# Softcap attention and a gated convolution block on one core: the first six pairs' steps and the weights' fetches placed anew

## The chip, the cores and the metric

The kernel runs on one core of one Trainium2 chip. The core's engines work side by side, each on its own list of instructions in order: TensorE (PE, the matmuls), ScalarE (ACT), VectorE (DVE), GpSimd (POOL) and SyncE (SP), which here issues all the transfers between the chip's memory and the core's own memory (SBUF). Matmuls write into PSUM, eight banks of it. The metric is the device time of one execution in microseconds (us); less is better.

## The reference: what is computed

For 8 batches, 12 heads, a sequence of 448 and a head size of 64:

```
scores = cap * tanh(q @ k^T / 8 / cap)          # 448 x 448 for each head
attn   = exp(scores - max) ; attn /= sum(attn) + 1e-9
x      = attn @ v                               # heads side by side: 448 x 768 for each batch
gate   = sigmoid(sum over i < 5 of conv_w[i] * x shifted by i - 4 rows)
out    = (gate * (x @ w_val)) @ w_out
```

q, k, v and cap are 32-bit floats; w_val, w_out (768 x 768 each) and conv_w (5 x 768) come as 64-bit floats, 8 bytes an element.

## The kernel before

Work goes by pairs of heads: 48 pairs, six to a batch. q and k come in blocks of 32 x 32 and are turned on DVE (`turn`, L296). `scores` (L317) gives four tiles a pair, each 112 keys by 448 queries for both heads; `tanh` (L325) and `exp` (L329) are ACT's. `attnv` (L354) multiplies exp'd tiles with v, and `sums` (L366) multiplies them with ones, which gives the denominators. DVE then turns the sums (L374), takes the reciprocal (L380, L381), spreads it (L387) and multiplies (L395): the result u is x for this pair, channels on partitions. `x_hi` (L400, ACT) and `x_lo` (L236, DVE) cut x into a leading and a remaining part. `conv` forms the gate's sum: its first product is ACT's (L412) for the first eleven pairs, the four others are DVE's (L416). For each batch there follow the value projection `val` (L437 to L439, three matmuls for each part of a product), the sigmoids (L422), the gate product (L443), and the output projection `out_part` (L466 to L468).

[...] Twelve steps of 256 rows by 384 columns (six for w_val, six for w_out) convert them during the first eleven pairs. A step fetches the same numbers twice (`weight_load`): as pairs of 32-bit words (`w_raw`, L270) and shifted by 16 bits (`w_late`, L271), in two pieces of 384 KB each. Then `float64_split` works in three parts: `first` is ACT's L136 and L137 on the raw copy, and DVE's L138 on the late copy; `second` is DVE's L141 and L142, which reads the raw copy for the last time; `third` is L145 and L146, which reads the late copy for the last time. There is one buffer for each copy and one for the work tile `w_t`, so a fetch for the next step must wait for L142 (raw) or L146 (late).

The order of the instructions on every engine is written out by hand. A table gives each step of a pair a time in units of a pair (`"tanh": (0.0, 0.01, 0.51, 0.52)` for the four tiles of pair p means p + 0.0 and so on); all steps of all pairs, with the weights' steps (`W_AT`), projections (`VAL_FIRST`, `OUT_EVEN` and so on) and sigmoids, are sorted by these times, and the engines' lists are made in that order. An engine takes its instructions in this order and waits at each until its inputs are there. There is no other planner: the times set the order alone.

Table `EARLY` serves pairs 0 to 4 and `HANDED` pair 5; pairs 6 to 10 have `PAIRED`, then `STEADY`, then `SPLIT`. In `EARLY`, pair p's ACT order is tanh 0, 1, exp 0, 1, tanh 2, 3, exp 2, 3, and then x_hi and the first convolution product of pair p-1. PE's is scores 2 and 3 of p, products and sums of tiles 2 and 3 of p-1, scores 0 and 1 of p+1, products and sums of tiles 0 and 1 of p. From pair 6 on, DVE first adds tiles two by two (L339), so that two sums a pair are left.

PSUM has two buffers for scores, each of two banks, two banks for products and sums of even pairs and, in the first six pairs, two (shared with the projections) for those of odd pairs (`bank`).

Of the kernel before, what the change touches and what calls it, by code (L numbers as in the profile page):

```python
# [10 lines left out]
U16 = mybir.dt.uint16  # L11

AF = mybir.ActivationFunctionType
ALU = mybir.AluOpType
# [7 lines left out]
P = 128  # L22
# [11 lines left out]
WC = 2  # L34
# [6 lines left out]
STEADY = {  # L41
    "load_q": -1.9,
    "load_k": -1.85,
    "load_v": -0.6,
    "tq": -0.90,
    "tk": -0.85,
    "scores": (0.0, 0.05, 0.62, 0.67),
    "tanh": (0.06, 0.13, 0.68, 0.75),
    "exp": (0.22, 0.29, 0.82, 0.89),
# [12 lines left out]
SPLIT = STEADY | {"q_hi": -0.69, "k_hi": -0.68, "q_lo": -0.475, "k_lo": -0.47}  # L62
PAIRED = STEADY | {"add": (0.52, 1.03), "sums": (1.28, 1.29)}
EARLY = {
    "load_q": -1.9,
    "load_k": -1.85,
    "load_v": -0.6,
    "tq": -0.78,
    "tk": -0.72,
    "scores": (-0.31, -0.30, 0.19, 0.20),  # L70
    "tanh": (0.0, 0.01, 0.51, 0.52),
    "exp": (0.17, 0.18, 0.68, 0.69),
    "av": (0.84, 0.95, 1.33, 1.46),
    "sums": (0.85, 0.96, 1.34, 1.47),
    "turn_sums": 1.60,
    "recip": 1.62,
    "spread": 1.65,
    "mul": 1.72,
    "x_hi": 1.87,
    "x_lo": 1.90,  # L80
    "conv": (1.88, 1.99, 2.06, 2.12, 2.18),
}

HANDED = EARLY | {
    "av": (0.84, 0.95, 1.06, 1.08),
    "sums": (0.85, 0.96, 1.07, 1.09),
    "turn_sums": 1.30,
    "recip": 1.32,
    "spread": 1.34,
    "mul": 1.40,  # L90
    "x_hi": 1.42,
    "x_lo": 1.46,
    "conv": (1.44, 1.54, 1.58, 1.70, 1.74),
}

LATE_X = {"x_lo": 1.76, "conv": (1.78, 1.80, 1.83, 1.86, 1.89)}
NEARLY, NPAIRED, NPLAIN = 6, 11, 13

VAL_FIRST = (6.50, 6.85, 7.36, 7.74, 8.36, 8.74)
VAL = (6.85, 7.36, 7.74, 8.36, 8.74, 9.36)  # L100
SIG_FIRST, SIG_AT = 7.15, 7.44
OUT_EVEN = (9.80, 10.36, 10.74, 11.36, 11.74, 12.36)
OUT_ODD = (9.80, 10.36, 10.74, 10.80, 11.36, 11.74, 11.80, 12.36)
OUT_LATE = (9.80, 10.36, 10.74, 11.74, 12.36, 12.60)
PART = 0.13
KEEP_AT = 10.2
W_AT = (0.93, 1.95, 2.9, 3.7, 4.5, 5.35, 7.1, 8.1, 9.1, 9.9, 10.6, 11.15)
W_LOAD = -0.5
W_SECOND, W_THIRD = 0.02, 0.05
W_FREE = 11.3  # L110
CW_LOAD, CW_AT = -0.55, 0.7
EPS = 1e-9


def words(ap):

    return ap.bitcast(I32).rearrange("p (n two) -> p n two", two=2)


def shifted(t, n):  # L120


    return t.bitcast(I32)[..., 1:2 * n:2]


def float64_split(nc, raw, mid, hi, lo, t):

    tf = t.bitcast(F32)
    top = raw[..., 1].bitcast(F32)

    def first():
        nc.scalar.activation(tf, top, AF.Copy, scale=2.0 ** -112)  # L136
        nc.scalar.sign(top, top)  # L137
        nc.vector.tensor_scalar(mid, mid, 0x01FFFFFF, None, ALU.bitwise_and)  # L138

    def second():  # L140
        nc.vector.tensor_scalar(t, t, 0x0FFFFE00, 3, ALU.bitwise_and, ALU.logical_shift_left)  # L141
        nc.vector.tensor_tensor(hi, tf, top, op=ALU.mult)  # L142

    def third():
        nc.vector.tensor_scalar(t, hi.bitcast(I32), -0x00800000, None, ALU.bitwise_and)  # L145
        nc.vector.scalar_tensor_tensor(lo, mid, 2.0 ** -36, tf, ALU.mult, ALU.mult)  # L146

    return first, second, third
# [39 lines left out]
def load_v(nc, pool, v, p):  # L188

    _, H, S, D = v.shape  # L190
    b, hp = divmod(p, H // 2)
    vn = pool.tile([CH, 2, S // CH, D], F32, name="vn")
    for j in range(2):
        nc.sync.dma_start(vn[:, j], v[b, 2 * hp + j].rearrange("(t r) d -> r t d", r=CH))
    return vn


def fast_path(tc, io, u2, q, k, v, w_val, conv_w, w_out, out, capt):
# [5 lines left out]
    nc = tc.nc  # L204
# [3 lines left out]
    NP = B * NPAIR  # L208
# [5 lines left out]
    NH = DM // 2  # L214
# [6 lines left out]
    with ExitStack() as ctx:  # L221
# [28 lines left out]
        for t in u2:  # L250
# [5 lines left out]
        wsteps = [  # L256
            (w, slice(c, c + WC), nh, t) for w, t in ((w_val, wv), (w_out, wo)) for nh in range(2) for c in range(0, NCC, WC)
        ]
        wstate = {}
# [3 lines left out]
        def weight_load(n):  # L263
            w, c, nh, _ = wsteps[n]
            raw = wsc.tile([P, WC, NH, 2], I32, name="w_raw", bufs=RB)
            late = wsc.tile([P, WC, 4 * NH + 2], U16, name="w_late", bufs=RB)
            for i in range(WC):
                r = (c.start + i) * P
                src = w[r:r + P, nh * NH:(nh + 1) * NH]
                nc.sync.dma_start(raw[:, i], words(src))  # L270
                nc.sync.dma_start(late[:, i, 1:1 + 4 * NH], src.bitcast(U16))  # L271
            wstate[n] = raw, shifted(late, NH)

        def weight_first(n):
            _, c, nh, w = wsteps[n]
# [18 lines left out]
        def turn(name, p):  # L294
            t = wk.tile([P, S], F32, name=name + "t")
            nc.vector.transpose(t, loads.pop((name, p)))  # L296
            state.setdefault(p, {})[name] = t
# [182 lines left out]
        stored = {}  # L480
        cw_steps = []
        events = []
        tables = [EARLY if p < NEARLY - 1 else HANDED if p < NEARLY else PAIRED if p < NPAIRED else STEADY if p < NPLAIN else SPLIT for p in range(NP)]
        for p in range(NPLAIN, NP):
            if p % NPAIR == 0:
                tables[p] = tables[p] | LATE_X
# [1 line left out]
        def at(when, f, *a):  # L488
            events.append((when, len(events), f, a))
# [4 lines left out]
            load_v=lambda p: vloads.update({p: load_v(nc, io, v, p)}),  # L494
            tq=lambda p: turn("q", p), tk=lambda p: turn("k", p),
            q_hi=lambda p: half_hi("q", p), k_hi=lambda p: half_hi("k", p),
            q_lo=lambda p: half_lo("q", p), k_lo=lambda p: half_lo("k", p),
            scores=scores, tanh=tanh, exp=exp, add=add, av=attnv, sums=sums, turn_sums=turn_sums, recip=norm_recip,
            spread=spread, mul=norm_mul, x_hi=x_hi, x_lo=x_lo, conv=conv,
        )  # L500
        for p, table in enumerate(tables):
            for name, f in steps.items():
                x = table.get(name, ())
# [5 lines left out]
        for b in range(B):  # L509
            t0 = NPAIR * b  # L510
# [14 lines left out]
            for m, y in enumerate(OUT_ODD if b % 2 else OUT_LATE if b == B - 2 else OUT_EVEN):  # L525
# [2 lines left out]
                at(t0 + y + 0.20, store, b, m)  # L528
                at(t0 + y + 0.40, store_out, b, m)
        for n, t0 in enumerate(W_AT):  # L530
            at(W_AT[n - 1] + W_THIRD if n else W_LOAD, weight_load, n)
            at(t0, weight_first, n)
            at(t0 + W_SECOND, weight_second, n)
            at(t0 + W_THIRD, weight_third, n)
        at(W_FREE, free_scratch)
        at(CW_LOAD, lambda: cw_steps.append(load_conv_w(nc, wsc, conv_w, cw)))
        at(CW_AT, lambda: cw_steps[0]())
# [129 lines left out]
def kernel(tc, q, k, v, cap, w_val, conv_w, w_out, out):  # L667
    nc = tc.nc
    with tc.tile_pool(name="cap_pool", bufs=1) as pool, tc.tile_pool(name="io", bufs=2) as io:
        capt = pool.tile([P, 1], F32, name="capt")  # L670
        nc.sync.dma_start(capt, cap.rearrange("(o c) -> o c", o=1).partition_broadcast(P))

        pad = conv_w.shape[0] - 1
        u2 = [pool.tile([P, pad + q.shape[2]], F32, name=f"u{i}") for i in range(2)]
        for t, src in zip(u2, (q, k)):
            load_blocks(nc, t[:, pad:], src, 0)
        mag = pool.tile([1, 1], F32, name="mag")
        nc.vector.scalar_tensor_tensor(mag, capt[0:1], -1.0, capt[0:1], ALU.mult, ALU.max)
        small = pool.tile([1, 1], I32, name="small")
        nc.vector.tensor_scalar(small, mag, CAP_FAST, None, ALU.is_le)  # L680
        flag = nc.values_load(small, min_val=0, max_val=1)
        with tc.If(flag != 0) as cmp:
            fast_path(tc, io, u2, q, k, v, w_val, conv_w, w_out, out, capt)
        with cmp.Else():
            general_path(tc, q, k, v, w_val, conv_w, w_out, out, capt)
# [30 lines left out]
```

## Time and profile before

| what | value |
|---|---|
| median of 3 runs | 774.95 us (773.33 to 777.27) |
| the profiled execution | 775.05 us, its span 773.3 us |
| mean granted clock of PE | 0.988 |
| busy share of the span | PE 95%, DVE 77%, ACT 70%, POOL 1% |
| HBM read, written | 51.94 MB, 11.01 MB |

A row of a timeline has the start from the span's beginning and the duration, both in us, then engine, line, operation, output and inputs, the shape and the count of instructions merged into the row; in brackets stands the engine's idle time just before it and who ended it. A row of waits has the waiting engine and line, what it waited for, and total us, count, and longest. A row of windows has for each engine the busy us and the instructions that began in the window; its last three columns are PE's granted clock, the share of the DMA engines' time, and GB/s. A row of DMA issues ends with KB each and median us from issue to landing. PE and PEld are the matmul and the weight-loading side of TensorE; a 32-bit matmul shows as two records, so one tile of scores for two heads is x4. PE's ends are modelled, so a busy PE need not be at its peak.

### The profile page before, as it was taken

The page shows a single profiled execution, that of the slowest core. Times are in us where ns is not written, and L with a number is a line of the kernel's source. Part 1 is how long each engine was busy: PE and PEld are TensorE (multiplying, and loading weights), DVE is VectorE, ACT ScalarE, POOL GpSimd, SP SyncE. Part 2 cuts the span into 40 slices and gives each one's busy share as a digit, 9 for nine tenths or more (in the row PEclk, how much of TensorE's full clock was granted, in tenths as well). Part 3 has the DMA queues.
Part 4 walks back from the last instruction along what each step waited for, and adds up shares of the span by engine and source line. Part 5 has one row for each costly group of instructions (what it writes and reads, how often), then busy time and mean ns, then how long its engine had stood idle before and what let it go on. Part 6 is the DMA issues. An engine that isn't in the chain of part 4 may idle for free.

```text
span 773.3 us, 10851 instructions
## 1 busy us (share of the span) xinstructions
PE 731.7 (95%) x3972; PEld 490.6 (63%) x3972; DVE 594.9 (77%) x972; ACT 538.8 (70%) x708; POOL 7.8 (1%) x16
## 2 busy tenths in 40 slices
PE   5787899999899999999999999999999999999997
PEld 1232356455676776676766777676666777575997
DVE  2688859878888778998898778998798778997510
ACT  4787677866877669767777669767777669766311
POOL 0000000100000000000000000000000000000000
PEclk9999999999999999999999999999999999999999
DMA  6888745484312333233322333234322333210001
GB/s 117 196 205 216 160 102 133 107 225 98 70 36 52 74 81 57 42 70 83 77 43 47 79 75 62 40 68 85 75 48 47 73 73 71 36 36 31 22 21 65
DMA packets 241820, 63.75 MB, mean 82 GB/s; under 512 B 228448, under 2 KB 235616, under 8 KB 241760
## 3 DMA queue, kind: packets, MB, share of 16 engines
q1 hardware_dynamic: 241760, 62.98, 37.1%
q8 instruction: 33, 0.54, 0.3%
q14 instruction: 27, 0.22, 0.1%
HBM read 51.94 MB, written 11.01 MB: 81 GB/s over the span
## 4 chain that ended last, share of the span: by engine, by line
PE 41%; DVE 20%; ACT 13%; issue 3%; DVEq 0%; ACTq 0%
PE psf L466 7%; PE pss L317 7%; PE psf L467 6%; PE psf L468 6%; PE psa L354 6%; DVE pa L339 4%; ACT pt L325 4%; ACT pt L329 4%; DVE gate L416 3%; PE psf L437 3%; PE psf L438 2%; PE psf L439 2%; ACT gate L422 2%; PE psz L366 2%; DVE g_l L236 1%
## 5 line engine op out<-in xcount | busy, mean ns | idle before, releaser
L325 ACT ACTIVATE pt<-pss,rc 112x896 f32<-112x896 f32 x192 | 186.0, 1005 | 35.4 <-PE pss L317 35.4
L329 ACT ACTIVATE pt<-pt,capt 112x896 f32<-112x896 f32 x192 | 189.2, 1038 | 0.1
L354 PE MATMUL psa<-pt,vn 112*64 112x448 f32 x720 | 147.7, 548 | 0.0
L416 DVE SCALAR_TENSOR_TENSOR gate<-u,cw,gate 128x448 f32<-128x448 f32 x192 | 132.3, 689 | 6.6 <-ACT gate L412 1.1
L466 PE MATMUL psf<-wo,g_h 128*128 128x384 f32 x336 | 117.8, 350 | 0.8 <-DVE wo L142 0.8
L437 PE MATMUL psf<-xh,wv 128*128 128x448 f32 x288 | 110.1, 382 | 5.8 <-DVE gate L443 3.1
L467 PE MATMUL psf<-wo,g_h 128*128 128x384 f32 x336 | 113.1, 337 | 1.1 <-DVE wo L146 1.1
L468 PE MATMUL psf<-wo,g_l 128*128 128x384 f32 x336 | 113.2, 337 | 0.0
L438 PE MATMUL psf<-xh,wv 128*128 128x448 f32 x288 | 105.3, 365 | 0.0
L439 PE MATMUL psf<-xl,wv 128*128 128x448 f32 x288 | 105.2, 365 | 0.0
L339 DVE TENSOR_TENSOR pa<-pt 112x896 f32<-112x896 f32 x84 | 91.1, 1084 | 16.1 <-ACT pt L329 16.1
L354 PEld LDWEIGHTS psa<-pt,vn 112*64 112x64 f32 x720 | 47.5, 137 | 82.3 <-issue 73.3
L400 ACT CAST xh<-u 128x448 fp32r<-128x448 f32 x48 | 27.1, 565 | 86.8 <-DVE u L395 86.8
L466 PEld LDWEIGHTS psf<-wo,g_h 128*128 128x128 f32 x336 | 63.5, 189 | 23.1 <-issue 17.8
L437 PEld LDWEIGHTS psf<-xh,wv 128*128 128x128 f32 x288 | 54.5, 189 | 34.0 <-issue 20.9
L374 DVE STREAM_TRANSPOSE zt<-psz 128x448 f32<-128x448 f32 x45 | 29.0, 644 | 60.2 <-PE psz L366 60.1
L317 PE MATMUL pss<-qt,kt 64*112 64x448 f32 x208 | 53.2, 630 | 22.8 <-ACT pt L325 14.2
L467 PEld LDWEIGHTS psf<-wo,g_h 128*128 128x128 f32 x336 | 63.6, 189 | 1.4 <-DVE wo L146 1.4
L468 PEld LDWEIGHTS psf<-wo,g_l 128*128 128x128 f32 x336 | 63.5, 189 | 0.3
L446 ACT CAST g_h<-gate 128x448 fp32r<-128x448 f32 x48 | 26.3, 562 | 48.5 <-DVE gate L443 48.3
L474 ACT COPY osb<-psf 128x384 f32<-128x384 f32 x56 | 26.8, 479 | 45.9 <-PE psf L468 45.9
L317 PE MATMUL pss<-qh,kh 64*112 64x448 f32 x280 | 58.5, 412 | 0.0
(74 smaller groups left out, 904.5 us busy)
## 6 DMA issues: line engine op xcount, KB each, us to landing
vn<-in_v_dram SPq DMA_DIRECT2D x96, 112.0 KB, 2.6
out_dram<-osb SPq DMA_DIRECT2D x56, 192.0 KB, 1.9
qn<-in_q_dram SPq DMA_DIRECT2D x188, 56.0 KB, 2.5
kn<-in_k_dram SPq DMA_DIRECT2D x188, 56.0 KB, 2.4
w_raw<-in_moe_w_val_dram SPq DMA_DIRECT2D x12, 384.0 KB, 4.6
w_late<-in_moe_w_val_dram SPq DMA_DIRECT2D x12, 384.0 KB, 5.1
w_raw<-in_moe_w_out_dram SPq DMA_DIRECT2D x12, 384.0 KB, 3.8
w_late<-in_moe_w_out_dram SPq DMA_DIRECT2D x12, 384.0 KB, 4.4
```

The lines of the kernel that those rows point to most:

```text
L317: nc.tensor.matmul(ps[:CH, j, :S], st[x][r, c], st[y][r], start=(n == 0), stop=(n == len(parts) - 1))
L325: nc.scalar.activation(st["p", i], st.pop(("s", i)), AF.Tanh, scale=rc8[:CH])
L329: nc.scalar.activation(t, t, AF.Exp, scale=capt[:CH])
L339: nc.vector.tensor_tensor(st["a", i], st["p", 2 * i], st["p", 2 * i + 1], op=ALU.add)
L354: nc.tensor.matmul(st["o"][r, :S], vloads[p][:, j, i], t[:, j], start=(i == 0), stop=(i == NKT - 1))
L416: nc.vector.scalar_tensor_tensor(g, u[:, i:i + S], cw[:, hp, i:i + 1], g, ALU.mult, ALU.add)
L437: nc.tensor.matmul(o, w_h, xh, start=(c == 0), stop=False)
L438: nc.tensor.matmul(o, w_l, xh, start=False, stop=False)
L439: nc.tensor.matmul(o, w_h, xl, start=False, stop=(c == NCC - 1))
L466: nc.tensor.matmul(o, g_h[:, d, s], w_h, start=(d == 0), stop=False)
L467: nc.tensor.matmul(o, g_h[:, d, s], w_l, start=False, stop=False)
L468: nc.tensor.matmul(o, g_l[:, d, s], w_h, start=False, stop=(d == NCC - 1))
```

## The change

It has four parts. For the first six pairs `EARLY` is new and `HANDED` is gone: products and sums of a pair's tiles 0 and 1 come behind its own scores 2 and 3, and those of tiles 2 and 3 behind the next pair's scores 0 and 1; the sums' transpose to u follows early in the next pair; x_hi and the first convolution product stand on ACT between the next pair's first and second half (1.30 instead of 1.87), x_lo and the other products behind them on DVE. Pair 6 has a table of its own (`SIXTH`): scores, tanh and exp as in `EARLY`, the rest as in `PAIRED`, with its adds earlier. In the conversion of weights L138 moves from the first to the third part; the two copies are fetched by two functions, the raw one behind the second part of the step before, the late one behind its third part; and the third part comes 0.71 of a pair behind the first (0.05 from step 6 on). Last, weight steps (`W_AT`), the first batch's sigmoids (`SIG_FIRST`) and the convolution weights (`CW_AT`) have other times.

```
 EARLY = {
...
-    "load_v": -0.6,
-    "tq": -0.78,
-    "tk": -0.72,
-    "scores": (-0.31, -0.30, 0.19, 0.20),
-    "tanh": (0.0, 0.01, 0.51, 0.52),
-    "exp": (0.17, 0.18, 0.68, 0.69),
-    "av": (0.84, 0.95, 1.33, 1.46),
-    "sums": (0.85, 0.96, 1.34, 1.47),
-    "turn_sums": 1.60,
-    "recip": 1.62,
-    "spread": 1.65,
-    "mul": 1.72,
-    "x_hi": 1.87,
-    "x_lo": 1.90,
-    "conv": (1.88, 1.99, 2.06, 2.12, 2.18),
+    "load_v": -0.7,
+    "tq": -0.72,
+    "tk": -0.70,
+    "scores": (-0.50, -0.49, 0.10, 0.11),
+    "tanh": (0.0, 0.01, 0.35, 0.36),
+    "exp": (0.17, 0.18, 0.52, 0.53),
+    "av": (0.28, 0.37, 0.65, 0.80),
+    "sums": (0.29, 0.38, 0.66, 0.81),
+    "turn_sums": 1.02,
+    "recip": 1.03,
+    "spread": 1.04,
+    "mul": 1.05,
+    "x_hi": 1.30,
+    "x_lo": 1.34,
+    "conv": (1.31, 1.50, 1.52, 1.54, 1.56),
 }
-HANDED = EARLY | {
...
+SIXTH = PAIRED | {k: EARLY[k] for k in ("tq", "tk", "scores", "tanh", "exp")} | {"add": (0.38, 0.62)}
...
-SIG_FIRST, SIG_AT = 7.15, 7.44
+SIG_FIRST, SIG_AT = 6.92, 7.44
...
-W_AT = (0.93, 1.95, 2.9, 3.7, 4.5, 5.35, 7.1, 8.1, 9.1, 9.9, 10.6, 11.15)
+W_AT = (0.70, 1.70, 2.70, 3.70, 4.70, 5.70, 7.1, 8.0, 8.9, 9.7, 10.4, 11.0)
...
-W_SECOND, W_THIRD = 0.02, 0.05
+W_SECOND, W_THIRD, W_THIRD_EARLY = 0.02, 0.05, 0.71
...
-CW_LOAD, CW_AT = -0.55, 0.7
+CW_LOAD, CW_AT = -0.55, 0.6
...
     def first():
         nc.scalar.activation(tf, top, AF.Copy, scale=2.0 ** -112)
         nc.scalar.sign(top, top)
-        nc.vector.tensor_scalar(mid, mid, 0x01FFFFFF, None, ALU.bitwise_and)
...
     def third():
+        nc.vector.tensor_scalar(mid, mid, 0x01FFFFFF, None, ALU.bitwise_and)
         nc.vector.tensor_scalar(t, hi.bitcast(I32), -0x00800000, None, ALU.bitwise_and)
...
         def weight_load(n):
             w, c, nh, _ = wsteps[n]
             raw = wsc.tile([P, WC, NH, 2], I32, name="w_raw", bufs=RB)
+            for i in range(WC):
+                r = (c.start + i) * P
+                nc.sync.dma_start(raw[:, i], words(w[r:r + P, nh * NH:(nh + 1) * NH]))
+            wstate[n] = raw
+
+        def late_load(n):
+            w, c, nh, _ = wsteps[n]
             late = wsc.tile([P, WC, 4 * NH + 2], U16, name="w_late", bufs=RB)
             for i in range(WC):
                 r = (c.start + i) * P
-                src = w[r:r + P, nh * NH:(nh + 1) * NH]
-                nc.sync.dma_start(raw[:, i], words(src))
-                nc.sync.dma_start(late[:, i, 1:1 + 4 * NH], src.bitcast(U16))
-            wstate[n] = raw, shifted(late, NH)
+                nc.sync.dma_start(late[:, i, 1:1 + 4 * NH], w[r:r + P, nh * NH:(nh + 1) * NH].bitcast(U16))
+            wstate[n] = wstate[n], shifted(late, NH)
...
-        tables = [EARLY if p < NEARLY - 1 else HANDED if p < NEARLY else PAIRED if p < NPAIRED else STEADY if p < NPLAIN else SPLIT for p in range(NP)]
+        tables = [EARLY if p < NEARLY else SIXTH if p == NEARLY else PAIRED if p < NPAIRED else STEADY if p < NPLAIN else SPLIT for p in range(NP)]
...
         for n, t0 in enumerate(W_AT):
-            at(W_AT[n - 1] + W_THIRD if n else W_LOAD, weight_load, n)
+            third = [x + (W_THIRD if x > NEARLY else W_THIRD_EARLY) for x in W_AT]
+            at(W_AT[n - 1] + W_SECOND if n else W_LOAD, weight_load, n)
+            at(third[n - 1] if n else W_LOAD, late_load, n)
             at(t0, weight_first, n)
             at(t0 + W_SECOND, weight_second, n)
-            at(t0 + W_THIRD, weight_third, n)
+            at(third[n], weight_third, n)
```

More of the change, by code (lines that the diff above doesn't have):

```diff
@@ L66 @@
     "load_k": -1.85,
-    "load_v": -0.6,
-    "tq": -0.78,
-    "tk": -0.72,
-    "scores": (-0.31, -0.30, 0.19, 0.20),
-    "tanh": (0.0, 0.01, 0.51, 0.52),
-    "exp": (0.17, 0.18, 0.68, 0.69),
-    "av": (0.84, 0.95, 1.33, 1.46),
-    "sums": (0.85, 0.96, 1.34, 1.47),
-    "turn_sums": 1.60,
-    "recip": 1.62,
-    "spread": 1.65,
-    "mul": 1.72,
-    "x_hi": 1.87,
-    "x_lo": 1.90,
-    "conv": (1.88, 1.99, 2.06, 2.12, 2.18),
-}
-HANDED = EARLY | {
[L85 to L94, printed above, removed]
+    "load_v": -0.7,
[13 more added lines that the diff above has]
+    "conv": (1.31, 1.50, 1.52, 1.54, 1.56),
+}
+SIXTH = PAIRED | {k: EARLY[k] for k in ("tq", "tk", "scores", "tanh", "exp")} | {"add": (0.38, 0.62)}
 LATE_X = {"x_lo": 1.76, "conv": (1.78, 1.80, 1.83, 1.86, 1.89)}
```

## The prediction

> **What bounds the kernel now.** I read the page first, then a table of windows, the waits of the first 160 us, and the timeline of each engine there.
>
> ```profile
> PE 731.7 (95%) x3972; PEld 490.6 (63%) x3972; DVE 594.9 (77%) x972; ACT 538.8 (70%) x708; POOL 7.8 (1%) x16
> ...
> vn<-in_v_dram SPq DMA_DIRECT2D x96, 112.0 KB, 2.6
> ...
> qn<-in_q_dram SPq DMA_DIRECT2D x188, 56.0 KB, 2.5
> ...
> w_raw<-in_moe_w_val_dram SPq DMA_DIRECT2D x12, 384.0 KB, 4.6
> w_late<-in_moe_w_val_dram SPq DMA_DIRECT2D x12, 384.0 KB, 5.1
> ```
>
> PE is busy for 95% of the span: over the whole program the matmuls are the bound, and only the 41.6 us in which PE has nothing to run (773.3 less 731.7) can be won. The change is in the first pairs, so the question is who ends last there. The waits of the stretch 0 to 160 us (total, count, longest):
>
> ```profile
> ACT xh L400 <- DVE u L395: 21.5, 10, 3.3
> PE pss L317 <- ACT pt L325: 14.2, 9, 3.7
> ...
> DVE w_late L138 <- DMA w_late<-in_moe_w_val_dram: 8.1, 5, 3.0
> ...
> ACT w_t L136 <- DMA w_raw<-in_moe_w_val_dram: 5.6, 2, 3.4
> ```
>
> Read from the bottom: ACT waits for a weight copy, VectorE (DVE) for the other one, ACT for the normalised rows u (its cast L400), and PE for the tanh L325 that frees a PSUM buffer. It is a ring: PE stands still because ACT does, and ACT because of u and of w_raw. ACT's timeline shows where:
>
> ```profile
> 20.32 0.89 ACT L136 ACTIVATE w_t<-w_raw 128x768 f32<-128x768 f32 x1 [2.25 <-DMA w_raw<-in_moe_w_val_dram]
> ...
> 22.02 1.89 ACT L325 ACTIVATE pt<-pss,rc 112x896 f32<-112x896 f32 x2
> ...
> 35.16 1.89 ACT L325 ACTIVATE pt<-pss,rc 112x896 f32<-112x896 f32 x2
> ...
> 46.68 1.90 ACT L325 ACTIVATE pt<-pss,rc 112x896 f32<-112x896 f32 x2
> ...
> 52.11 1.99 ACT L329 ACTIVATE pt<-pt,capt 112x896 f32<-112x896 f32 x2
> ...
> 57.33 0.56 ACT L400 CAST xh<-u 128x448 fp32r<-128x448 f32 x1 [0.39 <-DVE u L395]
> ...
> 58.37 1.88 ACT L325 ACTIVATE pt<-pss,rc 112x896 f32<-112x896 f32 x2
> ...
> 65.47 0.89 ACT L136 ACTIVATE w_t<-w_raw 128x768 f32<-128x768 f32 x1 [3.35 <-DMA w_raw<-in_moe_w_val_dram]
> ...
> 74.15 1.88 ACT L325 ACTIVATE pt<-pss,rc 112x896 f32<-112x896 f32 x2
> ...
> 86.35 1.89 ACT L325 ACTIVATE pt<-pss,rc 112x896 f32<-112x896 f32 x2
> ```
>
> The first tanh of pairs 1 to 6 starts at 22.02, 35.16, 46.68, 58.37, 74.15 and 86.35: pitches of 13.1, 11.5, 11.7, 15.8 and 12.2 us, 64.3 together. ACT's own work per pair is shorter: four rows of two, from 46.68 to 52.11 + 1.99, make 7.4 us of tanh and exp; cast and first product (57.33 to 58.37) 1.0; the weight step's two (20.32 to 22.02) 1.7. That is 10.2 us.
>
> DVE's work per pair:
>
> ```profile
> 52.05 0.64 DVE L296 STREAM_TRANSPOSE qt<-qn 128x448 f32<-128x448 f32 x1
> 52.61 0.60 DVE L296 STREAM_TRANSPOSE kt<-kn 128x448 f32<-128x448 f32 x1
> ...
> 66.97 0.56 DVE L138 TENSOR_SCALAR w_late<-w_late 128x768 int32<-128x768 int32 x1 [2.19 <-DMA w_late<-in_moe_w_val_dram]
> 67.44 0.55 DVE L141 TENSOR_SCALAR w_t<-w_t 128x768 int32<-128x768 int32 x1
> 68.09 0.96 DVE L142 TENSOR_TENSOR wv<-w_t,w_raw 128x768 fp32r<-128x768 f32 x1
> ...
> 70.55 0.64 DVE L374 STREAM_TRANSPOSE zt<-psf 128x448 f32<-128x448 f32 x1
> ...
> 72.45 0.62 DVE L395 TENSOR_TENSOR u<-psf,zt 128x448 f32<-128x448 f32 x1
> 73.71 0.63 DVE L236 TENSOR_TENSOR xl<-u,xh 128x448 fp32r<-128x448 f32 x1 [0.63 <-ACT xh L400]
> ...
> 147.45 2.84 DVE L416 SCALAR_TENSOR_TENSOR gate<-u,cw,gate 128x448 f32<-128x448 f32 x4
> ```
>
> Two transposes 1.2 (52.05 to 52.61 + 0.60); the weight step's five 3.6 (66.97 to 70.55); from the sums' transpose to u 2.5 (70.55 to 72.45 + 0.62); x_lo 0.6; four convolution steps 2.8. The sum is 10.7; neighbours overlap by about 0.1 where such pieces meet, so I take 10.6 us.
>
> PE, and the stretch behind the early pairs:
>
> ```profile
> 75.19 1.91 PE L317 MATMUL pss<-qt,kt 64*112 64x448 f32 x8 [0.42 <-ACT pt L325]
> ...
> 83.19 1.76 PE L317 MATMUL pss<-qt,kt 64*112 64x448 f32 x8
> ...
> 102.00 1.76 PE L317 MATMUL pss<-qt,kt 64*112 64x448 f32 x8
> ...
> 106.75 1.67 PE L366 MATMUL psz<-pa,ones 112*64 112x448 f32 x8
> 109.54 0.47 PE L437 MATMUL psf<-xh,wv 128*128 128x448 f32 x1 [1.12 <-DVE gate L443]
> ...
> 113.35 1.76 PE L317 MATMUL pss<-qt,kt 64*112 64x448 f32 x8
> ...
> 176.53 0.45 PE L466 MATMUL psf<-wo,g_h 128*128 128x384 f32 x1 [0.78 <-DVE wo L142]
> 178.12 0.44 PE L467 MATMUL psf<-wo,g_h 128*128 128x384 f32 x1 [1.14 <-DVE wo L146]
> ```
>
> From 75.19 to 83.19 PE runs two tiles of scores and four tiles of attention products and sums without a gap, 8.0 us; two more tiles of scores are 1.7: 9.7 us a pair. Last, the transfers (the queue's share over 20 to 90 us, and two windows whose last columns are PE's granted clock, DMA share, GB/s):
>
> ```profile
> q1 hardware_dynamic: 32957, 13.98, 86.0%
> ```
> ```profile
> 20.00:30.00 10.00, 6.93 (x26) 2.25 (x28) 4.82 (x8) 9.07 (x10) 0.00 (x0) 0.83 1.02 218
> 30.00:40.00 10.00, 8.37 (x44) 2.77 (x42) 8.44 (x15) 7.63 (x10) 0.00 (x0) 1.00 0.68 147
> ```
>
> Moving 13.98 MB took 0.86 of 70 us, 60.2 us. A pair needs four weight pieces of 384 KB, eight of 56 KB and two of 112 KB, 2.26 MB: 9.7 us. So DVE 10.6, ACT 10.2, PE 9.7, DMA 9.7 us: all below even the shortest pitch of 11.5. The early pairs are bound by waits, not by work.
>
> **The change, part by part.** I lay one pair out on a clock that is 0 when its first tanh starts.
>
> ACT: two tanh and two exp to 3.7; the cast and first product of the pair before, to 4.7; two tanh and two exp to 8.4; the weight step's two to 10.1. The added wait is the cast in the middle: behind it on ACT stand this pair's other tiles, and PE's next scores wait for those. It needs u of the pair before. On DVE, L142 (0.96) follows ACT's last weight instruction, at 0 to 1.0; transpose to u is 2.5 more: 3.5, just ahead of 3.7. So the cast's 21.5 us of waits mostly go; the slack is 0.2, and if u is late the delay passes straight into the pitch.
>
> DVE next: transposes to 4.7, x_lo to 5.3 (its 0.63 wait for the cast is covered by the transposes), the third weight step (L138, L145, L146: 3.6 less 1.6 for L141 and L142, 2.0) to 7.3, convolution to 10.1, L141 and L142 to 11.6: one turn is 10.6, longer than ACT's. DVE becomes the bound.
>
> PE: the products of tiles 0 and 1 now stand behind their own scores 2 and 3 and wait for their own exps (done at 2.8 and 3.7); behind them stand the next pair's scores. Scores 3 can start when the second tanh ends, 1.9, and last to 2.8; products and sums of two tiles take 3.1 (8.0 less 1.9, halved), to 5.9; the next scores need tanh 2 and 3, done by 6.6, and end at 7.6; the last two tiles to 10.7. The next scores 2 wait until 10.6 + 0.95. So PE idles about 0.9 us a turn, and ACT never waits for it.
>
> SP: the raw copy of the next step waits only for L142 (1.0) and is needed at 8.4: 7.4 us, against 4.6 to land and at most 1.0 to issue. The late copy waits for L146 (7.3) and is needed at 15.9: 8.6 us, against 5.1 and 1.0. Behind the late fetch's wait on SP stands the raw fetch, then q and k of two pairs on: these are not wanted for over a turn. So both weight waits (5.6 and 8.1 us) should go in the early pairs; what is late next is DVE.
>
> The start: weight step 0's second raw piece was issued third and landed near 20.3:
>
> ```profile
> 15.41 0.43 SPq L270 DMA_DIRECT2D w_raw<-in_moe_w_val_dram x1
> ```
>
> Now it is second, one slot of about 0.45 earlier and with one piece of 384 KB fewer ahead. The gain is between 0 and the 2.25 us wait at 20.32; of the 4.9 us to landing a third less is 1.6, and I take 1.4. Pair 1 starts at 20.6.
>
> Pair 6 then starts at 20.6 + 5 x 10.6 = 73.6 instead of 86.35.
>
> Behind it the order differs too: pair 5's products come before pair 6's first tanh is through, and all of pair 6's scores before the first value projection. From pair 6's start PE has: scores 3 done at 2.8; the first two value projections, 36 matmuls at 3.8 per 18 (109.54 to 113.35), 7.6; then scores, products and sums from 102.00 to 108.4, 6.4. That is 16.8, and the third projection starts, before at 109.54, now at 73.6 + 16.8 = 90.4: **19.1 us earlier**. DVE at that point still owes the third part of step 6, and the six sigmoids run ahead of pair 7's first tanh; by the same rows the gate products are done at about pair 6 + 13.5, before PE needs their PSUM buffers at 16.8, so I cost these moves at nothing. If that cover is gone, at most the 1.1 us of the row at 109.54 returns.
>
> The later weight steps come 0.1 to 0.2 pairs earlier: at best the two waits at 176.53 and 178.12 go (1.9 us); at worst denser steps on DVE cost as much as 3. I take 0.
>
> Sum: 775.05 (profiled execution, span 773.3) - 19.1 = 755.95. The median of the runs, 774.95, is 0.1 below that execution, so I say **756.0 us**.
>
> [...] In the window 20 to 30 PE is granted 0.83, in 30 to 40, with 1.6 us idle in several pieces, 1.00. [...]
>
> **Rivals.**
> - *The fetches stay late.* Both copies still go through one SP queue and the same 16 engines, so splitting them moves nothing, and each turn keeps the shortest pitch seen, 11.5. For: 0.86 of the DMA time is used. Against: 7.4 us of room for 4.6. Pair 6 at 78.1, time 760.5.
> - *PE's clock dips in every turn.* At 0.83 its 9.7 us become 11.7, above DVE's 10.6: pair 6 at 79.1, time 761.5. For: the window 20 to 30. Against: the window 30 to 40.
> - *Given back later.* Denser weight steps on DVE in pairs 7 to 11 cost 3: 759.
> - *Half and half.* The cast waits for u again in most turns, pitch about 13.8: 772.
> - *Slower than before.* The late copy closes a loop: L146, issue, landing, L138, L145, L146. By the rows it is 1.0 + 5.1 + 2.0 = 8.1 us. It binds when landing takes over 7.6, and the kernel loses from a pitch of 14.4 (landing 11.4). If every turn were like that from 58.37 to 74.15, 15.8, pair 6 would start at 99.6 and the time be 782. Against: the median landing is 5.1.
>
> **How the numbers follow.** Forecast 0.68; fetches late 0.17; clock 0.07; given back 0.03; half and half 0.03; slower 0.02. A measurement of this kernel can tell about 0.5%, 3.9 us. The first four are faster by more: 0.95; half and half is same: 0.03; slower 0.02. Low end: pitch 10.2, whole start wait gone, both late waits gone: pair 6 at 70.8, 751. High end: pitch 11.5, no gain at the start, 3 lost later: 765.
>
> **What would show it.** Right: first tanhs of pairs 1 to 6 about 10.6 us apart; no DMA behind L136 or L138 before 70 us; L400's wait below 0.5 each; granted clock 1.00 from 30 on; the third value projection near 90. Wrong: a pitch above 11.5 with L136, L138 or L400 waiting, or new PE gaps above 2 us in pairs 7 to 11.

## The result, and the profile after

| | before | changed |
|---|---|---|
| median of 4 runs | 774.91 us (773.33 to 777.27) | 754.88 us (752.42 to 757.62) |
| profiled execution, its span | 775.05 us, 773.3 us | 752.42 us, 750.7 us |
| mean granted clock of PE | 0.988 | 0.997 |

The ratio is 0.9759, 95% interval 0.9719 to 0.9799 (the quotient of the two medians, 0.9742, lies inside it). The forecast was 756.0, with a range of 751 to 765. Line numbers have moved in the changed kernel: tanh is L320, exp L324, cast L395, u L390, sums' transpose L369, weight steps L126 and L127 (ACT), L130 and L131 (second), L134 to L136 (third), scores L312, products L349, sums L361, adds L334.

The page's first line:

```profile
PE 725.2 (97%) x3972; PEld 487.0 (65%) x3972; DVE 592.8 (79%) x972; ACT 538.1 (72%) x708; POOL 7.5 (1%) x16
```

The work of DVE and ACT is what it was (594.9 to 592.8, 538.8 to 538.1); PE has 25.5 us with nothing to run instead of 41.6. PE's busy time fell too, by 6.5 us for the same 3972 matmuls. Most of that lies ahead of the third value projection. The windows up to it, first the kernel before and then the changed one, hold the same 372 matmuls:

```profile
0.00:109.50 109.50, 84.93 (x372) 32.29 (x372) 71.87 (x129) 77.32 (x93) 0.66 (x8) 0.95 0.72 162
```
```profile
0.00:90.50 90.50, 79.83 (x372) 31.00 (x372) 68.84 (x126) 78.62 (x96) 0.66 (x8) 1.00 0.86 191
```

PE is busy 5.1 us less there, at a granted clock of 1.00 instead of 0.95, and idle 13.9 us less. The first tanhs of pairs 1 to 6 on ACT's timeline:

```profile
20.94 1.89 ACT L320 ACTIVATE pt<-pss,rc 112x896 f32<-112x896 f32 x2
...
31.21 1.89 ACT L320 ACTIVATE pt<-pss,rc 112x896 f32<-112x896 f32 x2
...
43.17 1.89 ACT L320 ACTIVATE pt<-pss,rc 112x896 f32<-112x896 f32 x2
...
53.40 1.91 ACT L320 ACTIVATE pt<-pss,rc 112x896 f32<-112x896 f32 x2
...
63.64 1.90 ACT L320 ACTIVATE pt<-pss,rc 112x896 f32<-112x896 f32 x2
...
73.89 1.91 ACT L320 ACTIVATE pt<-pss,rc 112x896 f32<-112x896 f32 x2
```

The pitches are 10.3, 12.0, 10.2, 10.2 and 10.3 us, where they were 13.1, 11.5, 11.7, 15.8 and 12.2. The waits of the stretch 20 to 85 us:

```profile
DVE zt L369 <- PE psf L361: 1.8, 1, 1.8
ACT xh L395 <- DVE u L390: 1.7, 1, 1.7
PE pss L312 <- ACT pt L320: 1.6, 5, 0.4
...
ACT w_t L126 <- DMA w_raw<-in_moe_w_val_dram: 1.1, 1, 1.1
```

ACT waits once for a weight copy (the very first), DVE never for w_late, and the cast once for u; PE's five waits for tanh are 0.4 at most. From one transpose of the sums to the next a pair later, DVE now runs without a gap:

```profile
34.11 0.65 DVE L369 STREAM_TRANSPOSE zt<-psf 128x448 f32<-128x448 f32 x1 [1.81 <-PE psf L361]
...
44.36 0.64 DVE L369 STREAM_TRANSPOSE zt<-psz 128x448 f32<-128x448 f32 x1
...
54.60 0.65 DVE L369 STREAM_TRANSPOSE zt<-psf 128x448 f32<-128x448 f32 x1
```

That is 10.24 us a turn; the 1.81 in the first row is the turn of 12.0. In the turn that starts at 43.17, DVE's u and ACT's cast that takes it:

```profile
46.26 0.62 DVE L390 TENSOR_TENSOR u<-psa,zt 128x448 f32<-128x448 f32 x1
```
```profile
46.92 0.56 ACT L395 CAST xh<-u 128x448 fp32r<-128x448 f32 x1
```

PE's rows for the turn of 12.0, for the third value projection, and for the longest wait that is left behind it:

```profile
25.16 1.42 PE L349 MATMUL psf<-pt,vn 112*64 112x448 f32 x3 [1.27 <-ACT xh L395]
...
90.56 0.47 PE L432 MATMUL psf<-xh,wv 128*128 128x448 f32 x1
...
124.43 1.08 PE L361 MATMUL psz<-pa,ones 112*64 112x448 f32 x4 [2.35 <-DVE pa L334]
```

The third projection starts at 90.56 instead of 109.54: 19.0 of the two executions' 22.6 us are won by then. From there to the end it is 660.1 us instead of 663.8.

### The profile page after: what moved, and what is told of

Same layout as the page of the kernel before. It is cut to its first block, busy times and chain, and to the rows that moved or that the text cites. A ratio compares the mean times of both kernels' runs of the same rounds, so it can differ in the third digit from the quotient of the medians.

```text
span 750.7 us, 10859 instructions
## 1 busy us (share of the span) xinstructions
PE 725.2 (97%) x3972; PEld 487.0 (65%) x3972; DVE 592.8 (79%) x972; ACT 538.1 (72%) x708; POOL 7.5 (1%) x16
## 4 chain that ended last, share of the span: by engine, by line
PE 44%; DVE 24%; ACT 24%; issue 5%; SPq 2%; DMA 1%; DVEq 0%; ACTq 0%
ACT pt L320 7%; PE psf L461 7%; PE pss L312 7%; ACT pt L324 6%; PE psf L463 6%; PE psf L462 6%; PE psa L349 6%; DVE pa L334 5%; DVE gate L411 3%; ACT gate L417 3%; PE psf L432 3%; PE psz L361 2%; PE psf L434 2%; PE psf L433 2%; DVE g_l L226 2%
## 5 line engine op out<-in xcount | busy, mean ns | idle before, releaser
L320 ACT ACTIVATE pt<-pss,rc 112x896 f32<-112x896 f32 x192 | 185.8, 1004 | 29.0 <-PE pss L312 29.0
L324 ACT ACTIVATE pt<-pt,capt 112x896 f32<-112x896 f32 x192 | 189.3, 1039 | 0.1
L349 PE MATMUL psa<-pt,vn 112*64 112x448 f32 x720 | 147.7, 546 | 0.0
L432 PE MATMUL psf<-xh,wv 128*128 128x448 f32 x288 | 108.9, 378 | 2.1 <-DVE gate L438 2.0
L433 PE MATMUL psf<-xh,wv 128*128 128x448 f32 x288 | 104.3, 362 | 0.0
L334 DVE TENSOR_TENSOR pa<-pt 112x896 f32<-112x896 f32 x84 | 91.1, 1084 | 12.6 <-ACT pt L324 12.6
L349 PEld LDWEIGHTS psa<-pt,vn 112*64 112x64 f32 x720 | 47.7, 136 | 81.2 <-issue 69.8
L395 ACT CAST xh<-u 128x448 fp32r<-128x448 f32 x48 | 27.1, 565 | 76.8 <-DVE u L390 76.7
L461 PEld LDWEIGHTS psf<-wo,g_h 128*128 128x128 f32 x336 | 63.0, 188 | 22.6 <-issue 18.3
L369 DVE STREAM_TRANSPOSE zt<-psz 128x448 f32<-128x448 f32 x45 | 28.9, 642 | 57.1 <-PE psz L361 57.0
L312 PE MATMUL pss<-qt,kt 64*112 64x448 f32 x208 | 50.6, 606 | 9.6 <-DVE guard L235 7.8
L312 PE MATMUL pss<-qh,kh 64*112 64x448 f32 x280 | 58.5, 412 | 0.0
```

Of the source, the lines that this page charges most:

```text
L312: nc.tensor.matmul(ps[:CH, j, :S], st[x][r, c], st[y][r], start=(n == 0), stop=(n == len(parts) - 1))
L320: nc.scalar.activation(st["p", i], st.pop(("s", i)), AF.Tanh, scale=rc8[:CH])
L324: nc.scalar.activation(t, t, AF.Exp, scale=capt[:CH])
L334: nc.vector.tensor_tensor(st["a", i], st["p", 2 * i], st["p", 2 * i + 1], op=ALU.add)
L349: nc.tensor.matmul(st["o"][r, :S], vloads[p][:, j, i], t[:, j], start=(i == 0), stop=(i == NKT - 1))
L432: nc.tensor.matmul(o, w_h, xh, start=(c == 0), stop=False)
```

## The experiments

The median of the kernel before was 773.62, 772.43 and 772.94 in the three sets of runs, so ratios are compared. "Pair 6" is the start of its first tanh (86.35 before, 73.89 changed).

**fetch_together**: the raw copy's fetch moves to the late copy's place, ahead of it.

```
-            at(W_AT[n - 1] + W_SECOND if n else W_LOAD, weight_load, n)
+            at(third[n - 1] if n else W_LOAD, weight_load, n)
```

> The changed kernel with one part undone: the raw copy of the next step is again fetched behind the third part, together with the late copy. Theory (the early pairs are bound by waits, and the split of the fetches is what takes the raw wait off ACT): in the changed kernel the third part ends 7.2 us behind a pair's first tanh; issue 0.9 and landing 4.5 bring the raw copy to 12.6, ACT wants it at 8.4, and its two instructions take 1.7: pitches of about 14.3 us instead of 10.25, 4.2 us of wait for w_raw in each turn, pair 6 starting near 95 instead of 73.9, and a time of about 773. Rival (both copies go through one SP queue and the same 16 engines, so the moment of issue matters little, and the new order alone gives the gain): pitches of 10.3 to 11.5, time 753 to 761.

Measured: 757.83 us, ratio 0.9796 (0.9766 to 0.9826); one wait of 4.6 for w_raw in the first turn, later ones of 0 to 1.2; pair 6 at 79.21. The expectation's theory was wrong about this edit: SP's list is an order, and a fetch waited only for its buffer (in the second turn the raw copy went out at 39.25, the late one only at 42.82). The raw copy, ahead of the late one, still waited for L131 alone and was late only by q, k and v ahead of it: in the first turn it went out at 28.25 instead of 23.29.

**fetch_as_before**: one function again, raw, late, raw, late, at the third part's place, so that the second raw piece stands behind the late copy's wait.

```
             for i in range(WC):
                 r = (c.start + i) * P
-                nc.sync.dma_start(late[:, i, 1:1 + 4 * NH], w[r:r + P, nh * NH:(nh + 1) * NH].bitcast(U16))
+                src = w[r:r + P, nh * NH:(nh + 1) * NH]
+                nc.sync.dma_start(raw[:, i], words(src))
+                nc.sync.dma_start(late[:, i, 1:1 + 4 * NH], src.bitcast(U16))
...
-            at(W_AT[n - 1] + W_SECOND if n else W_LOAD, weight_load, n)
-            at(third[n - 1] if n else W_LOAD, late_load, n)
+            at(third[n - 1] if n else W_LOAD, weight_load, n)
```

> The changed kernel with the fetches as before: one function issues raw, late, raw, late at the place of the third part. In the run named fetch_together the raw copy stood ahead of the late one and waited only for L131, so it was late by its place behind q, k and v alone; here its second piece stands behind the late copy's wait for the third part (L136). Theory (the raw copy's loop: weight step on ACT, L131 1.0, to u 2.5, transposes and x_lo 1.7, third part 2.0, issue 0.9, landing 4.5, weight step 1.7): pitches of 13.3 to 14.3, 3 to 4 us of wait for w_raw in each turn, pair 6 at 87 to 92, time 766 to 773. Rival (fetch_together took 757.8, so where the copies are issued costs a few us and no more): pitches under 11.5, time 756 to 761.

Measured: 772.82 us, ratio 1.0006 (0.9983 to 1.0028): the whole gain is gone. ACT's timeline and SP's:

```profile
49.12 0.92 ACT L126 ACTIVATE w_t<-w_raw 128x768 f32<-128x768 f32 x1 [2.87 <-issue]
62.12 0.89 ACT L126 ACTIVATE w_t<-w_raw 128x768 f32<-128x768 f32 x1 [2.82 <-DMA w_raw<-in_moe_w_val_dram]
75.45 0.93 ACT L126 ACTIVATE w_t<-w_raw 128x768 f32<-128x768 f32 x1 [3.17 <-DMA w_raw<-in_moe_w_val_dram]
```
```profile
53.13 0.44 SPq L260 DMA_DIRECT2D w_raw<-in_moe_w_val_dram x1
57.95 0.35 SPq L261 DMA_DIRECT2D w_late<-in_moe_w_val_dram x1
58.35 0.42 SPq L260 DMA_DIRECT2D w_raw<-in_moe_w_val_dram x1
```

The first raw piece goes out at 53.13, the second only at 58.35, behind the late piece's wait, and ACT takes it at 62.12, 3.8 us later. The first turn is 15.7 long, the other four 13.0 to 13.4, about 3 us of each ACT waiting. The loop is real, and the split is what breaks it: the raw copy must not stand behind the late copy's wait.

**old_order**: the order before with the new weights' part (the sigmoids and late weight steps in their old places too).

```
-EARLY = {   # the new tables, SIXTH
+EARLY = {   # the tables before, HANDED
...
-SIG_FIRST, SIG_AT = 6.92, 7.44
+SIG_FIRST, SIG_AT = 7.15, 7.44
...
-W_AT = (0.70, 1.70, 2.70, 3.70, 4.70, 5.70, 7.1, 8.0, 8.9, 9.7, 10.4, 11.0)
+W_AT = (0.70, 1.70, 2.70, 3.70, 4.70, 5.70, 7.1, 8.1, 9.1, 9.9, 10.6, 11.15)
```

> The changed kernel with the steps of the first seven pairs, the first sigmoids and the later weight steps in the old order; the split fetches, L138 in the third part and the third part 0.71 of a pair late stay. Theory (the order takes away the waits of the cast for u): the waits for w_raw and w_late are gone, but the cast still waits for u, which before cost ACT 2.9, 1.3, 0.4, 2.2 and 2.0 us in five turns, 1.8 a turn; pitches of 10.2 + 1.8 = 12 us, pair 6 near 80, time about 768. Rival (the weights' copies were the whole cause): pitches of 10.3 to 10.6, pair 6 near 74, time 757 or less.

Measured: 757.79 us, ratio 0.981 (0.9762 to 0.9858). Pitches 11.5, 10.7, 10.9, 10.8 and 10.5:

```profile
42.82 1.88 ACT L330 ACTIVATE pt<-pss,rc 112x896 f32<-112x896 f32 x2
...
53.70 1.87 ACT L330 ACTIVATE pt<-pss,rc 112x896 f32<-112x896 f32 x2
...
64.54 1.88 ACT L330 ACTIVATE pt<-pss,rc 112x896 f32<-112x896 f32 x2
...
75.03 1.89 ACT L330 ACTIVATE pt<-pss,rc 112x896 f32<-112x896 f32 x2
```
```profile
79.81 0.47 PE L442 MATMUL psf<-xh,wv 128*128 128x448 f32 x1 [1.32 <-DVE zt L379]
...
97.40 0.47 PE L442 MATMUL psf<-xh,wv 128*128 128x448 f32 x1 [1.46 <-DVE gate L448]
```

My theory failed here. At 0.70 the weight step stands on ACT ahead of the old place of the cast, and its 1.8 us cover the time that u needs: in these turns the cast does not wait, and ACT waits for w_raw instead, 0.3 to 1.3 us a turn. (That the third part on DVE stands later may help u as well; no run parts the two.) The new weights' part alone brings pair 6 to 75.03. What is left for the new order is 1.1 us in the turns and, behind pair 6's start, 22.4 us to the third projection (97.40) against 16.7: 6.8 us. Behind that the old order has 658.9 us left, the changed kernel 660.1, so a little of it is given back. These are single executions; the two ratios, 0.981 and 0.9759, have intervals that overlap.

**old_weights**: the new order with the early weight steps as before.

```
-W_AT = (0.70, 1.70, 2.70, 3.70, 4.70, 5.70, 7.1, 8.0, 8.9, 9.7, 10.4, 11.0)
+W_AT = (0.93, 1.95, 2.9, 3.7, 4.5, 5.35, 7.1, 8.0, 8.9, 9.7, 10.4, 11.0)
...
-W_SECOND, W_THIRD, W_THIRD_EARLY = 0.02, 0.05, 0.71
+W_SECOND, W_THIRD, W_THIRD_EARLY = 0.02, 0.05, 0.05
```

(L138's operation is back in `first`, and the fetches are those of fetch_as_before.)

> The new order of the first seven pairs alone: fetches as before, L138 in the first part, the third part right behind the second, the first six weight steps at their old times (two of them in the middle of a pair); the later steps stay at their new times. With old_order (757.8) it divides the change in two. Theory (the weights' part carries most of the gain, since it is in old_order already, and the order needs it: with the weight step of 3.6 us in one piece ahead of the transpose of the sums, u comes 1.5 to 2 us late for the cast in the middle of ACT's list, and the raw copy has less room): pitches of 12 to 13, pair 6 at 81 to 86, time 762 to 768. Rival (either part alone is enough, each takes away a cover that the other would take too): pitches of 10.5 to 11, pair 6 near 75, time 753 to 758.

Measured: 768.17 us, ratio 0.9949 (0.9919 to 0.9979); the third projection at 100.34. The cast waits for u in every turn, 1.4 to 2.2 us (9.1 in five), as the theory had it. So of the 2.4% the weights' part alone is worth 1.9% and the order alone 0.5%.

**tiles01_late**: products of tiles 0 and 1 behind the next pair's scores.

```
-    "av": (0.28, 0.37, 0.65, 0.80),
-    "sums": (0.29, 0.38, 0.66, 0.81),
+    "av": (0.56, 0.58, 0.65, 0.80),
+    "sums": (0.57, 0.59, 0.66, 0.81),
```

> The changed kernel with one part undone: in the first six pairs the products of tiles 0 and 1 stand behind the next pair's scores 0 and 1 again, in front of those of tiles 2 and 3. Theory (u is ready in time only because half the products are done early): PE stands idle between scores 3 and the next scores, then does all four tiles' products, and u comes late; the loop is cast and product 1.0, two tanh 1.9, one tile of scores 0.9, four tiles of products and sums 6.2, transpose to u 2.5, about 12.6 us a turn; ACT's cast waits about 2.3 us in each turn, pair 6 starts near 86, time about 765. Rival (PE has 0.3 to 0.9 us to spare in a turn, and the order of products inside it doesn't matter): pitch 10.25 to 10.6, time 752 to 757.

Measured: 774.28 us, ratio 1.0011 (0.9997 to 1.0026); pair 6 at 90.48. The direction is the theory's, but behind a first turn of 11.7 the other four are 14.2 to 15.6, not 12.6. ACT, PE, and a window (its third column from the end is PE's granted clock):

```profile
69.75 0.57 ACT L395 CAST xh<-u 128x448 fp32r<-128x448 f32 x1 [4.13 <-DVE u L390]
```
```profile
57.51 2.74 PE L312 MATMUL pss<-qt,kt 64*112 64x448 f32 x8 [3.01 <-ACT pt L320]
```
```profile
57.00:62.00 5.00, 4.49 (x14) 1.39 (x16) 4.86 (x8) 4.97 (x7) 0.00 (x0) 0.66 0.41 134
```

PE stands for 3.0 us, then runs at a granted clock of 0.66: the scores take 2.74 instead of 1.9, and the first four products behind them 1.69, where the next four take 0.92. The same stop of 3.0 us stands in all five turns, and the scores behind it take 2.7 to 3.3. The wait cost twice here.

**cast_late**: the cast and what hangs on it behind the second half's exps.

```
-    "x_hi": 1.30,
-    "x_lo": 1.34,
-    "conv": (1.31, 1.50, 1.52, 1.54, 1.56),
+    "x_hi": 1.60,
+    "x_lo": 1.62,
+    "conv": (1.61, 1.63, 1.64, 1.65, 1.66),
```

> The changed kernel with x_hi, x_lo and the convolution products of the pair before put behind the second half's exps (1.60 to 1.66) instead of between the halves. Theory (a turn is as full as DVE, and DVE only needs something to do: the cast's place shifts its work, once): pitches stay near 10.3, one slip of 2 to 4 us at the start or at the first value projection, which waits for pair 5's x_lo; time 756 to 759. Rival (the cast in the middle is what shortens the turn): DVE waits about 2.1 us for the cast in each turn, pitches about 12, time about 763 to 766.

Measured: 755.84 us, ratio 0.9774 (0.9722 to 0.9826); pitches 10.1, 12.5 (a wait of 2.1 for w_raw), 10.1, 10.1 and 11.3 (a wait of 1.0 for DVE's gate), pair 6 at 74.69. The cast's place in the middle is not what shortens the turn. It does matter behind: in the first value projections PE stands 1.8 us for the cast, and the matmuls behind that are 0.37 apart instead of 0.2 for some 3 us, so that from pair 6 to the third projection it is 20.8 us instead of 16.7.

**dve_more** and **act_more**: half a microsecond more for one engine in each early pair.

```
+            for _ in range(2 if p < NEARLY else 1):
                 less(nc.vector, xl, gates[p][1][:, PAD:PAD + S], xs[p])
...
+            for _ in range(2 if p < NEARLY else 1):
                 nc.scalar.copy(xh, gates[p][1][:, PAD:PAD + S])
```

> The changed kernel with x_lo computed twice in the first six pairs (the same values written again): 0.5 us more on DVE in each turn, nothing else. Theory (DVE is the bound of a turn: from one row to the same row a pair later it runs 10.24 us without a gap): pitches of pairs 3 to 6 go from 10.24 to 10.75, pair 6 comes about 2.5 later. Rival (ACT alone sets the pitch, DVE has room): 10.24 as before.

> The changed kernel with the cast x_hi made twice in the first six pairs (the same values written again): 0.47 us more on ACT in each turn. Theory (DVE is the bound and ACT waits only 0.1 us for u in a turn, so ACT is nearly as full): pitches of pairs 3 to 6 go from 10.24 to 10.6, 0.35 to 0.4 more. Rival (ACT has real room): at most 10.3. Together with dve_more: if both cost their full duration, the turn is full on both engines.

DVE's transposes of the sums with dve_more, and ACT's first tanhs with act_more:

```profile
44.24 0.64 DVE L369 STREAM_TRANSPOSE zt<-psz 128x448 f32<-128x448 f32 x1
...
55.14 0.64 DVE L369 STREAM_TRANSPOSE zt<-psf 128x448 f32<-128x448 f32 x1
...
66.03 0.64 DVE L369 STREAM_TRANSPOSE zt<-psz 128x448 f32<-128x448 f32 x1
```
```profile
53.88 1.91 ACT L320 ACTIVATE pt<-pss,rc 112x896 f32<-112x896 f32 x2
...
64.62 1.89 ACT L320 ACTIVATE pt<-pss,rc 112x896 f32<-112x896 f32 x2
```

DVE's turn goes from 10.24 to 10.9, by the whole of the added instruction (two take 1.24 where one took 0.58); ACT's addition makes it 10.74, about 0.1 less than its own length of 0.56. Both engines are full. Pair 6 comes at 75.14 and 75.34, 1.25 and 1.45 later, where 2.5 was expected for dve_more: in that run the start and the first two turns were 0.8 us shorter, and the last turn was 10.2. (One run each: 754.26 and 754.51 us; four such turns are within what single runs differ by.)

**v_early**: v of pair 1 ahead of q and k of pair 2.

```
+        tables[1] = tables[1] | {"load_v": -0.95}
```

> The changed kernel with the v of pair 1 fetched ahead of q and k of pair 2 instead of behind them. In the changed kernel one pitch of the five is long: pairs 1 to 2 take 10.3, pairs 2 to 3 take 12.0, the others 10.25, because PE's first product of pair 1 starts at 25.16 after 1.27 us idle, and the sums of pair 1 end late, so that DVE waits 1.8 and ACT's cast 1.7. Theory: that product waits for v, whose fetch was issued at 22.2 to 23.2 behind a slow k. With v early it starts at 23.8, all five pitches are 10.2 to 10.4, and pair 6 starts near 72.2 instead of 73.9; the span falls by about 1.7 us, which one time can't show. Rival (PE waits there for ACT's cast, as the row names it, or is late for another reason): the product starts at 25.1 as before, and pair 6 at 73.9.

```profile
23.59 0.97 PE L349 MATMUL psf<-pt,vn 112*64 112x448 f32 x4
...
33.76 1.49 PE L349 MATMUL psa<-pt,vn 112*64 112x448 f32 x3
```

The product that had waited now starts at 23.59 with no idle time, so its wait was for v, as the theory has it; the row of the changed kernel names ACT's cast, which only ended at the same moment. But pair 6 stays at 73.92: the turn behind it is 11.1, and w_raw is waited for by 0.4 and 0.6 in two later turns. In that turn the second row, three records in 1.49 where the first has four in 0.97, is the next pair's; its v was issued only at 29.34 to 31.60, behind q and k, so it probably had to wait for v within the group. One run: 754.36 us.

**second_later** and **second_later_v**: second and third part of weight steps 7 to 9 later on DVE; in the second also all early v ahead of q and k (`"load_v": -0.95` in `EARLY`).

```
+            second = [x + (0.13 if 7.5 < x < 10 else W_SECOND) for x in W_AT]
+            third = [y + 0.03 if x > NEARLY else x + W_THIRD_EARLY for x, y in zip(W_AT, second)]
```

> The changed kernel with one thing more: the second and third parts of weight steps 7, 8 and 9 stand 0.11 of a pair later on DVE, behind the gate products and the adds of tiles, instead of right behind the ACT part. In the changed kernel PE waits 0.65 at 106.19 and 2.35 at 124.43 for the adds, because DVE stands 1.1 to 1.7 us and then 0.4 at L130 and L131 for ACT's weight step, with the adds queued behind; PE's clock is granted 0.83 in the window behind the longer wait. Theory (these waits are DVE's order alone): both waits go, 3 to 4 us less than the changed kernel, time about 751. Rival (DVE is full in this stretch, as in the pairs before, so that the wait moves to another place): 754 to 755, with PE waiting elsewhere between 105 and 160.

> second_later with v of the next pair fetched ahead of q and k in all of the first six pairs (in v_early it was pair 1's alone). Theory: in v_early the product of pair 1 no longer waited, but v of pair 2, behind q and k, then landed late; with all of them ahead, no pitch has a wait for v, the long pitch of 12.0 between pairs 2 and 3 shrinks to 10.3, and pair 6 starts near 72.2, 1.7 earlier; time 1 to 2 below second_later. Rival (the transfers are full enough in these pairs that what is put ahead makes another late): some pitch stays above 10.8 with a wait for w_raw or for u behind q and k, time equal to second_later.

Measured: 756.03 us, ratio 0.9782 (0.9747 to 0.9817), and 757.06, 0.9788 (0.9755 to 0.982). No gain. In second_later the waits at 106 and 124 are gone, and in their place stands, on PE:

```profile
130.43 1.84 PE L312 MATMUL pss<-qt,kt 64*112 64x448 f32 x4 [3.49 <-ACT pt L320]
```

The rival was right that the wait moves; its reason, that DVE is full there, is not shown, as the row names ACT. With all v ahead no product waits for v, but the long turn is still 11.4, with the cast waiting 1.2 for u, w_raw is waited for by 0.5 and 0.3, and pair 6 comes at 73.92 all the same: here too the rival was right.

**late_steps_old**: the last six weight steps at 7.1, 8.1, 9.1, 9.9, 10.6 and 11.15.

> The changed kernel with the last six weight steps at their old times (7.1, 8.1, 9.1, 9.9, 10.6, 11.15). Theory: the two waits of the output projection for wo that the kernel before had at 176.5 and 178.1 (1.9 us) return, so 1 to 3 more than the changed kernel: 756 to 758. Rival: the order around them is another now, the old times cost nothing or gain (they keep the step off the adds): 752 to 755.

Measured: 751.67 us (751.29 to 752.42), ratio 0.9718 (0.9677 to 0.9759), the lowest of all. It beats the kernel before; its interval overlaps that of the changed kernel, so between these two the runs do not decide. All four of its runs have a granted clock of 0.997, which only one of the changed kernel's four has (the others 0.994 to 0.995). The waits for wo do not return, against my theory: they had gone with the earlier part.

## Why the prediction was right

- *"The early pairs are bound by waits, not by work."* Shown: the work of DVE and ACT stayed, pair 6 starts 12.5 us earlier, and either undoing (fetch_as_before, tiles01_late) brings a wait back and takes the whole gain.
- *"only the 41.6 us in which PE has nothing to run ... can be won."* Wrong: of the 22.6 us between the profiled executions 16.1 came from PE's idle time and 6.5 from its busy time, with a mean granted clock of 0.997 instead of 0.988. The forecast did not suffer, because it counts from where the kernel before stood at 109.54, slow matmuls included.
- *"DVE becomes the bound", 10.6 a turn.* Shown by dve_more; the size is 10.24, since the pieces of my sum overlap by more than the 0.1 that I took off. ACT is nearly as full, which the prediction did not have: it gave ACT 10.1 of 10.6, half a microsecond to spare, and act_more leaves it 0.1.
- *Five equal turns.* Wrong by one: the turn of 12.0 waits for v of pair 1. My account of SP's list has q and k behind the weights, "not wanted for over a turn", and leaves v out. The new table asks for the products 0.56 of a pair earlier (0.28 instead of 0.84) and for v only 0.1 earlier, still behind q and k of the next pair; v_early shows that this was the wait. This +1.4 and four turns of -0.35 cancel, and the start was 20.94 for 20.6: 73.89 for 73.6. The right sum has two errors in it.
- *16.8 us from pair 6 to the third projection*: measured 16.7, with no stop on PE between the scores and the projections.
- *The later steps, "I take 0".* The sum, between the profiled executions, was 19.1 against 22.6; the term that is off is this one: 3.6 us less. Part of that is luck of the execution: the profiled one was the fastest of the four, and by the medians the gain is 20.0. PE is busy 1.4 us less there and idle 2.2 us less (sums of the windows behind the third projection). The waits at 176.5 and 178.1 went, one of 2.31 at 156.24 (for the adds) shrank to 1.11, one of 2.35 at 124.43 came, and one dip of PE's clock is missing (below). late_steps_old shows that the later times are not the cause.
- *"L142 (0.96) follows ACT's last weight instruction, at 0 to 1.0 ... just ahead of 3.7."* It came so, but closer: u ends at 46.88, 3.71 us into its turn instead of 3.5, and the cast starts at 46.92. As an account of why the cast's waits go it was only half of it. With the weight step ahead of the cast, the old order has no wait either (old_order), and with the cast late the turns are as short (cast_late) and the time is the same within the intervals. What the new order adds lies mostly behind pair 6's start, as far as single executions show.
- *Rivals.* The fetches were not late, but would have been without the split. The clock did not dip in the turns: with stops of 0.3 to 0.4 us it stayed at 1.00 from 30 to 120. It fell where the stop was 3.0 us (0.66 from 57 to 62, tiles01_late). Nothing came near the slow loop.
- *"What would show it."* Most of the signs came as named, but two of those named for "wrong" came once each: a turn above 11.5 with the cast waiting (12.0, waiting 1.7), and a stop of PE above 2 us in pairs 7 to 11 (2.35). And L136 (now L126) waited once for its copy, 1.05 us, in the first step. None of these spread to the other turns.

What stays open: runs of one kernel differ by up to 5 us (752.42 to 757.62), which hides differences of 2 or 3 between these versions. Much of it goes with PE's granted clock: of the 44 runs of the kernel before in the three sets, the two at 0.983 took 779.2 and 779.5 us, the fifteen at 0.988 took 772.9 to 775.6, and the two at 0.995 took 768.2 and 772.6. What gives a run its clock is not shown.

## What to carry to other kernels

Lay one turn of the loop on a clock for each engine, and add up every loop through a buffer (last read, issue, landing, first use) beside the engines' sums; here the split of the fetches decides over the whole gain (fetch_as_before), because without it one such loop, 13 us, is longer than any engine's 10.2. A place behind a wait in SP's queue cost far more here than a place behind other transfers (ratio 1.0006 against 0.9796): ask what stands ahead, not where the line is written. Include every transfer that the new order wants earlier; here v was missed. With ACT and DVE full to 0.1 us, a further move of one step (v_early) only moved the wait.

## What the runs showed of the hardware that was not expected

PE's granted clock fell behind some stops and not behind others, and the length of the stop did not settle it. It fell behind 2.35 us (0.83 from 120 to 130 in the changed kernel) and 3.0 us (0.66 from 57 to 62 in tiles01_late); behind 1.8 us in cast_late the matmuls from 84.11 to 87.09 took 0.57 instead of 0.36 us; behind 1.27 us, at 25.16 in the changed kernel, it stayed at 1.00. Stops of 1.99 us went both ways. Before the change a stop of 1.99 us at 211.25 is followed by a window at 0.83, and eight matmuls, from 211.88 to 214.86, take 0.58 instead of 0.36 us; the changed kernel has the same stop, 1.99 us at 190.43, and its clock stays at 1.00. The kernel before:

```profile
211.25 0.47 PE L437 MATMUL psf<-xh,wv 128*128 128x448 f32 x1 [1.99 <-DVE gate L443]
```
```profile
210.00:220.00 10.00, 8.75 (x42) 6.40 (x44) 7.97 (x13) 7.65 (x10) 0.00 (x0) 0.83 0.01 2
```

The changed kernel:

```profile
190.43 0.47 PE L432 MATMUL psf<-xh,wv 128*128 128x448 f32 x1 [1.99 <-DVE gate L438]
```
```profile
191.00:201.00 10.00, 10.00 (x56) 6.44 (x55) 8.58 (x15) 9.73 (x13) 0.00 (x0) 1.00 0.09 21
```

The same stop cost some 1.3 us in one execution (eight matmuls 0.37 apart instead of 0.2) and nothing in the other; no run here shows why.
